# Attention into gated products: six token groups of 384 across batches instead of eight of 256 and 320

## The chip, the core and the metric

The kernel runs on one core of a Trainium2 chip. The metric is device time in microseconds (us). The engines are TensorE (PE; its weight loads are listed as PEld), VectorE (DVE), ScalarE (ACT), GpSimd (POOL) and SyncE (SP, which issues most DMAs).

## The reference

Three stages follow each other on 2304 tokens (4 batches of 576), in float32:

```python
scores = q @ k.T / 8                                  # 4 batches, 8 heads, 576 x 576, head dim 64
thresh = max(scores, -1) - tau
p = softmax(where(scores >= thresh, scores, -1e9))    # p / (sum + 1e-9)
x = (p @ v) as (2304, 512)
x = ((x @ w1) * (x @ w2) @ w3) @ w_out                # 512 -> 1024 -> 1024 -> 512
out = leaky(x @ w_in, 0.01) @ w_out2                  # 512 -> 2048 -> 512
```

## The kernel before

**Numbers.** Large products are made of float32r parts: a value is split into hi (a cast on ScalarE) and lo (value minus hi, on DVE or POOL), and each product takes three passes, hi hi, hi lo and lo hi (`PASSES`). Weights arrive as 64-bit words and are decoded in halves of 512 columns: ScalarE, DVE and POOL each have work in every half (L133 to L157).

**Attention.** Work goes by units: one batch, one pair of heads, one group of queries. A batch has two groups (`GROUPS`): queries 0 to 255 in two chunks of 128, and queries 256 to 575 as a tail of 64 (chunk `None`, both heads together) and two chunks of 128. A step is one chunk (`STEPS`, 80 in all, 64 chunks and 16 tails). In step n the kernel masks and normalises step n (`mask`), makes the scores of step n+1 (`scores`: matmuls, maximum on DVE, exponential on ScalarE), and transposes step n (`transposes`: four 128x128 transposes for each head into one PSUM tile `tp`, copied into `HH` by ScalarE for one head and by DVE for the other, and the ends of both heads through `tq` into `tl`). `mask` reads the scores in PSUM, and the score tiles are single, so the scores of the next step begin only when the mask of the one before has read them. The first 8 units (`PER`) use float32 scores, the later ones split q and k (`split_unit`). One step after a unit's last, `weighted` multiplies v^T by e (20 PE instructions, `av`) and splits the result out of PSUM into `x` (L349 on ScalarE, L350 on DVE).

**Filler.** The gated product of a group of tokens (`gated`) needs `x` of its four pairs of heads. It makes 16 sums of 12 matmuls (`psab`, L422), multiplies the two of each block (L430), splits the product into `gt` (L432, and L433 on POOL), and makes 4 sums of 24 matmuls (`psh`, L441), which go to DRAM as `h3d`. It is a generator that yields after each 12 matmuls (24 pieces a group). Two steps after the last step of a group it becomes the filler, and later steps draw pieces at 1.22 or 1.55 a unit of weight (a chunk weighs 2, a tail 1) at three places: behind `weighted`, between the two transposes, and behind them. Before the first group is ready, the places hold 16 pieces that fold w3 and w_out into `w34` (L388, 8 PE instructions each, two a step); a piece waits until the halves that it needs were decoded in earlier steps, and `load_halves` asks for 4 halves a step of the 40. Dummy matmuls (`keep_busy`, L496) run in the first three steps.

**Order.** The PE runs in the order in which the program is written. ACT, DVE and POOL are ordered by a planner in the attention part, and as written from the last gated group on. There, the last group's pieces (`last`) have no attention beside them; the work that prepares the second stage (`first_h3`, `prepare_up`, `prepare_down`) is drawn piece by piece beside them.

**Second stage.** 24 rounds of `products` (L861, 42 matmuls of 384 columns) and `down` (L896, 36 of 512 columns).

Of the kernel before, what the change touches and what calls it, by code (L numbers as in the profile page):

```python
# [44 lines left out]
def attention_gated_ffn(ctx: ExitStack, tc: tile.TileContext, qkv, tau, w3t, wout, w12, w2, out):  # L45
# [19 lines left out]
    xpool = s_ffn.enter_context(tc.tile_pool(name="xpool", bufs=6, reuse_waits="tile"))  # L65
# [95 lines left out]
    units = [(b * 4 + p, g) for b in range(B) for g in range(2) for p in range(4)]  # L161
    qk_t, vv_t = {}, {}

    def load_unit(u):

        if u >= len(units):
            return
        pair, g = units[u]
        gq, gw, _ = GROUPS[g]
        b, h = pair // 4, 2 * (pair % 4)  # L170
        qk = apool.tile([P, KS + 320], F32, tag="qk", name="qk", bufs=3)
        for a in range(2):
            o = a * D
            src = qkv[b, h + a][o:o + D]
            if g == 0:
                nc.sync.dma_start(out=qk[o:o + D, D:KS + gw], in_=src[:, :S + gw])
            else:
                nc.sync.dma_start(out=qk[o:o + D, D:KS], in_=src[:, :S])
                nc.sync.dma_start(out=qk[o:o + D, KS:], in_=src[:, S + gq:2 * S])
# [3 lines left out]
    def load_v(u):  # L183
        if u >= len(units):
            return
        pair = units[u][0]
        b, h = pair // 4, 2 * (pair % 4)
# [7 lines left out]
    def scale_unit(u):  # L195
# [3 lines left out]
        g = units[u][1]  # L199
        qk = qk_t[u]  # L200
        if g:
            for a in range(2):
                o = a * D
                tc.keep_in_program_order(nc.vector.tensor_scalar(
                    out=qz[u % 2][o:o + D, o:o + D], in0=qk[o:o + D, KS:KS + D], scalar1=scl[o:o + D],
                    scalar2=None, op0=ALU.mult))
        q = qk[:, KS + (D if g else 0):KS + GROUPS[g][1]]
# [5 lines left out]
    def split_unit(u):  # L213

        if not PER <= u < len(units):
            return
        g = units[u][1]
        n = KS + GROUPS[g][1]
# [9 lines left out]
        if g:  # L228
            for i, part in enumerate((hi, lo)):
                for a in range(2):  # L230
                    r = slice(a * D, a * D + D)
                    nc.vector.tensor_copy(qzs[u % 2][r, i, r], part[r, KS:KS + D])
# [4 lines left out]
    def scores(n):  # L237

        pair, g, c = STEPS[n]
        u = units.index((pair, g))  # L240
# [3 lines left out]
        if u < PER:  # L244
            parts, qzu = (qk,), qz[u % 2].unsqueeze(1)
        else:
            parts, qzu = qks_t[u], qzs[u % 2]
        passes = PASSES[:1] if u < PER else PASSES
        for half in range(2):
            for i, (x, y) in enumerate(passes):  # L250
                for a in heads:
                    if c is None:
                        lhs, rhs = qzu[:, x], parts[y][:, D + half * HS:D + half * HS + HS]
                    else:
                        r = slice(a * D, a * D + D)
                        o = KS + Q0[c] - GROUPS[g][0]
# [5 lines left out]
        nms = apool.tile([P, 2], F32, tag="nm", name="nm", bufs=4)  # L262
        th = apool.tile([P, 2], F32, tag="th", name="th", bufs=4)
# [8 lines left out]
        sc_t[n], e_t[n] = (sc, [th[:, a:a + 1] for a in heads]), e  # L272

    def mask(n):
        pair, g, c = STEPS[n]
        sc, ths = sc_t.pop(n)
        st = apool.tile([P, 2], F32, tag="stat", name="stat", bufs=4)
# [19 lines left out]
    def transposes(n):  # L297
# [3 lines left out]

        pair, g, c = STEPS[n]
        if (pair, g) not in he_t:
            he_t[pair, g] = apool.tile([P, 4, 2, 320], F32, tag="HH", name="HH")
        HH, tail = he_t[pair, g], tl[pair % 2]
# [14 lines left out]
        o = Q0[c] - GROUPS[g][0]  # L320
# [15 lines left out]
    def weighted(pair, g):  # L336

        gw = GROUPS[g][1]
        vv = vv_t[units.index((pair, g))]
        HH, tail = he_t.pop((pair, g)), tl[pair % 2]  # L340
# [646 lines left out]
```

## Time and profile before

| | us |
|---|---|
| median of 3 runs (lowest, highest) | 1034.69 (1030.94, 1035.38) |
| the profiled execution | 1033.24 |
| its span, first to last instruction | 1031.5 |
| PE busy | 1006.1 (98%) |
| DVE busy | 638.6 (62%) |
| ACT busy | 565.4 (55%) |
| POOL busy | 239.2 (23%) |

The mean granted clock of TensorE is 0.997 of full speed. Durations of single matmuls overlap, since they are pipelined; the distance from one start to the next is what a matmul costs when the PE is never idle. The chain that ended last goes mostly through L896 and L861, the second stage.

### The profile page before, as it was taken

What the parts mean: (1) busy time and instruction counts of PE and PEld (TensorE: products, weight loads), DVE (VectorE), ACT (ScalarE), POOL (GpSimd) and SP (SyncE); (2) the same over time, 40 slices, a digit from 0 to 9 for tenths busy, and PEclk for the clock granted to TensorE, in tenths of its full rate; (3) what the DMA queues carried; (4) which work ended last, traced back from release to release, by engine and by line L of the source; (5) the groups of instructions that cost most, each with busy time, mean ns of one, the idle gap of its engine ahead of it and who ended that gap; (6) DMA issues with size and microseconds to landing.
All of it is one profiled execution on the core that took longest, in us unless ns stands there. A gap on an engine that the chain in (4) does not pass through costs nothing. (4 is left out here: it accounts for less than half of the span.)

```text
span 1031.5 us, 17439 instructions
## 1 busy us (share of the span) xinstructions
PE 1006.1 (98%) x6472; PEld 862.6 (84%) x6472; DVE 638.6 (62%) x1394; ACT 565.4 (55%) x1084; POOL 239.2 (23%) x235
## 2 busy tenths in 40 slices
PE   7999899999999999999999999999999999999998
PEld 5555588889888888888898899998988999999997
DVE  7888788776787667887767856476683111621111
ACT  5778755554565545565545646677874333543332
POOL 2556510010110110100101135344552111411110
PEclk9999999999999999999999999999999999999999
DMA  8666211312121212112110225678645952064401
GB/s 291 229 218 218 69 50 40 108 43 62 44 59 53 62 37 62 49 44 69 45 49 20 73 83 188 225 300 281 211 147 194 424 195 95 1 242 192 189 1 62
DMA packets 53284, 129.59 MB, mean 126 GB/s; under 512 B 15824, under 2 KB 31184, under 8 KB 49360
## 3 DMA queue, kind: packets, MB, share of 16 engines
q1 hardware_dynamic: 53056, 128.48, 36.2%
q8 instruction: 51, 0.84, 0.3%
q14 instruction: 33, 0.27, 0.1%
q10 hardware_dynamic: 144, 0.00, 0.0%
HBM read 95.95 MB, written 32.51 MB: 125 GB/s over the span
## 5 line engine op out<-in xcount | busy, mean ns | idle before, releaser
L422 PE MATMUL psab<-x,w 128*128 128x256 f32 (+1 forms) x1536 | 232.4, 302 | 2.0 <-DVE w L394 0.5
L422 PEld LDWEIGHTS psab<-x,w 128*128 128x128 f32 x1536 | 208.7, 189 | 18.4 <-issue 10.3
L896 PE MATMUL po<-dn,gg 128*128 128x512 f32 x864 | 222.9, 390 | 0.0
L896 PEld LDWEIGHTS po<-dn,gg 128*128 128x128 f32 x864 | 160.1, 188 | 22.0
L861 PE MATMUL ps<-h,uph 128*128 128x384 f32 x672 | 172.9, 339 | 1.4 <-DVE sum L843 0.6
L267 ACT ACTIVATE e<-sc,nm 128x576 f32<-128x576 f32 x144 | 100.9, 738 | 82.8 <-DVE nm L266 81.9
L266 DVE TENSOR_REDUCE nm<-sc 128x1 f32<-128x576 f32 x144 | 103.2, 752 | 65.5 <-PE sc L259 65.4
L843 DVE TENSOR_TENSOR sum<-snap,ps 128x384 f32<-128x384 f32 x72 | 39.8, 552 | 167.1 <-PE ps L861 157.0
L861 PEld LDWEIGHTS ps<-h,uph 128*128 128x128 f32 x672 | 123.4, 188 | 15.7 <-DVE sum L843 1.4
L433 POOL TENSOR_TENSOR gt<-at,gt 128x256 fp32r<-128x256 f32 (+1 forms) x64 | 52.5, 820 | 340.2 <-ACT gt L432 340.0
L280 DVE SCALAR_TENSOR_TENSOR e<-sc,th,e 128x576 f32<-128x576 f32 x144 | 113.2, 814 | 12.5 <-ACT e L267 8.9
L441 PE MATMUL psh<-gt,w 128*128 128x256 f32 (+1 forms) x768 | 114.9, 301 | 1.3 <-POOL gt L433 1.3
L861 PE MATMUL ps<-h,upl 128*128 128x384 f32 x336 | 113.2, 337 | 0.0
L441 PEld LDWEIGHTS psh<-gt,w 128*128 128x128 f32 x768 | 103.9, 189 | 6.5 <-issue 3.5
L851 POOL TENSOR_TENSOR gg<-sum,gg 128x384 fp32r<-128x384 f32 x48 | 50.5, 1052 | 248.1 <-ACT gg L850 230.3
L325 PE MATMUL tp<-ident,e 128*128 128x128 f32 x512 | 78.5, 276 | 10.9 <-ACT HH L331 10.0
L838 ACT COPY snap<-ps 128x384 f32<-128x384 f32 x72 | 34.3, 476 | 86.8 <-PE ps L861 86.6
L325 PEld LDWEIGHTS tp<-ident,e 128*128 128x128 f32 x512 | 61.2, 142 | 21.5 <-ACT HH L331 14.0
L346 PE MATMUL av<-HH,vv 128*64 128x256 f32 (+1 forms) x512 | 67.6, 406 | 0.0
L848 ACT ACTIVATE sum<-sum 128x384 f32<-128x384 f32 x72 | 37.8, 525 | 48.1 <-DVE sum L843 48.1
L861 PEld LDWEIGHTS ps<-h,upl 128*128 128x128 f32 x336 | 63.1, 188 | 0.0
L291 ACT ACTIVATE e<-e,stat 128x576 f32<-128x576 f32 x64 | 49.7, 777 | 23.8 <-DVE stat L285 23.5
(116 smaller groups left out, 1399.2 us busy)
## 6 DMA issues: line engine op xcount, KB each, us to landing
st<-in_w SPq DMA_DIRECT2D x48, 512.0 KB, 5.9
dn<-dn_d SPq DMA_DIRECT2D x10, 1024.0 KB, 7.2
uph<-up_d SPq DMA_DIRECT2D x10, 896.0 KB, 9.2
upl<-up_d SPq DMA_DIRECT2D x10, 896.0 KB, 4.6
vv<-in_qkv SPq DMA_DIRECT2D x64, 128.0 KB, 2.1
raw<-in_w3t SPq DMA_DIRECT2D x8, 1024.0 KB, 7.6
dn_d<-dn SPq DMA_DIRECT2D x8, 1024.0 KB, 6.9
up_d<-uph SPq DMA_DIRECT2D x8, 896.0 KB, 4.6
```

Of the source, the lines that this page charges most:

```text
L266: nc.vector.tensor_reduce(out=nm, in_=sc[a][:, :, :HS], op=ALU.max, axis=AX.XY, negate=True)
L267: nc.scalar.activation(e[:, a * S:a * S + S].rearrange("p (a b) -> p a b", a=2), sc[a][:, :, :HS], AF.Exp, bias=nm)
L280: nc.vector.scalar_tensor_tensor(out=ev, in0=sc[a][:, :, :HS], scalar=th, in1=ev, op0=ALU.is_ge, op1=ALU.mult, accum_out=st[:, a:a + 1])
L291: nc.scalar.activation(ev, ev, AF.Copy, scale=st[:, a:a + 1])
L325: nc.tensor.transpose(tp[:, kc], e[:, k0:k0 + P], ident)
L346: nc.tensor.matmul(av[a * D:a * D + D, :gw], vv[:, a, kc], rhs, start=(i == 0), stop=(i == NK - 1))
L422: nc.tensor.matmul(ps[:, :gw], w12_t[i][:, a, mat * 512 + kk * P:mat * 512 + kk * P + P], xt[kk][:, c, :gw], start=(m == 0), stop=(m == 11))
L433: nc.gpsimd.tensor_tensor(out=gt[i][:, 1, :gw], in0=at[:, :gw], in1=f(gt[i][:, 0, :gw]), op=ALU.subtract)
L441: nc.tensor.matmul(ps[:, :gw], w34_t[i // 2][:, a, i % 2, o * P:o * P + P], gt[i][:, c, :gw], start=(m == 0), stop=(m == 23))
L851: eng.tensor_tensor(out=gg[:, 1], in0=gf, in1=f(gg[:, 0]), op=ALU.subtract)
L861: nc.tensor.matmul(ps, (uph, upl)[a][:, wi, i * P:i * P + P], hs[k][:, c, i], start=(opens[k] and m == 0), stop=(m == 5), skip_group_check ...
L896: nc.tensor.matmul(po_t[o], gg[:, c, t * P:t * P + P], dn[:, i, a], start=(q == 0 and seen[o] == 1 and m == 0), stop=(q == NQ - 1 and seen ...
```

## The change

The queries of two batches that follow each other (1152 tokens) are cut into three groups of 384. The first is queries 0 to 383 of the even batch in three chunks; the second joins its last 192 (a tail of 64 and one chunk) to the first 192 of the odd batch (likewise); the third is the last 384 of the odd batch. There are 32 units and 80 steps as before, with 384 or 192 queries to a unit. The gated product runs for 6 groups of 384 tokens, each matmul 384 columns wide. `weighted` only copies `av` into a float32 tile `xr` of the group (on ScalarE); `split_x` makes hi and lo of all four tiles in front of `gated`. A gated generator yields after 6 matmuls (48 pieces a group), and says whether a sum is open; open sums are finished ahead of `weighted`. The rate is 2.04, `load_halves` asks for 3 halves a step, `qz`, `tl` and `qzs` are single, intermediate tiles of the last group come from `fpool` too, the first two rings of the second stage trade places, and preparation for it is drawn at every second piece. The rest of the diff (not shown) puts the new names and widths in place of the old ones.

```diff
-Q0 = (0, 128, 320, 448)
-GROUPS = ((0, 256, (0, 1)), (HF, 320, (2, 3)))
 NK = 5
-CHUNKS = ((0, 1), (None, 2, 3))
-STEPS = tuple(
-    (b * 4 + p, g, c) for b in range(B) for g in range(2) for p in range(4) for c in CHUNKS[g])
+GW = 384
+NG = NT // GW
+PARTS = (
+    ((0, 384, (0, 128, 256)), (384, 192, (None, 64))),
+    ((0, 192, (None, 64)), (192, 384, (0, 128, 256))))
+UNITS = tuple(
+    (b + i, p, g) for b in range(0, B, 2)
+    for several in (((0, 0),), ((0, 1), (1, 0)), ((1, 1),)) for p in range(4) for i, g in several)
+STEPS = tuple((u, c) for u, (b, p, g) in enumerate(UNITS) for c in PARTS[b % 2][g][2])
...
-    xpool = s_ffn.enter_context(tc.tile_pool(name="xpool", bufs=6, reuse_waits="tile"))
+    xpool = s_ffn.enter_context(tc.tile_pool(name="xpool", bufs=4, reuse_waits="tile"))
...
-    qz = [apool.tile([P, P], F32, name=f"qz{i}") for i in range(2)]
-    tl = [apool.tile([P, 320], F32, name=f"tl{i}") for i in range(2)]
+    qz = apool.tile([P, P], F32, name="qz")
+    tl = apool.tile([P, GW], F32, name="tl")
     vvs = [apool.tile([P, 2, NK, D], F32, name=f"vv{i}") for i in range(2)]
-    for t in (*qz, *tl, *(vv[:, :, NK - 1] for vv in vvs)):
+    for t in (qz, tl, *(vv[:, :, NK - 1] for vv in vvs)):
         nc.vector.memset(t, 0.0)
-    qzs = [apool.tile([P, 2, P], F32R, name=f"qzs{i}") for i in range(2)]
-    for t in qzs:
-        nc.vector.tensor_copy(t, tl[0][:, :2 * P].rearrange("p (a w) -> p a w", a=2))
+    qzs = apool.tile([P, 2, P], F32R, name="qzs")
+    nc.vector.tensor_copy(qzs, tl[:, :2 * P].rearrange("p (a w) -> p a w", a=2))
...
+    def piece_of(u):
+
+        b, p, g = UNITS[u]
+        gq, gw, blocks = PARTS[b % 2][g]
+        at = b * S + gq
+        return gq, gw, blocks[0] is None, at // GW, at % GW
...
+        few = apool.tile([P, 6], F32, tag="nm", name="nm", bufs=4)
+        nms, th = few[:, :2], few[:, 2:4]
...
-        x = x_t[pair, g] = xpool.tile([P, 2, 320], F32R, tag="x", name="x")
-        nc.scalar.copy(x[:, 0, :gw], av[:, :gw])
-        nc.vector.tensor_tensor(
-            out=x[:, 1, :gw], in0=av[:, :gw], in1=f(x[:, 0, :gw]), op=ALU.subtract)
-
+        if (gid, p) not in x_t:
+            x_t[gid, p] = xpool.tile([P, GW], F32, tag="xr", name="xr")
+        nc.scalar.copy(x_t[gid, p][:, at:at + gw], av[:, :gw])
+
+    def split_x(gid):
+
+        xt = []
+        for p in range(KD):
+            raw = x_t.pop((gid, p))
+            x = xpool.tile([P, 2, GW], F32R, tag="x", name="x")
+            nc.scalar.copy(x[:, 0], raw)
+            nc.vector.tensor_tensor(out=x[:, 1], in0=raw, in1=f(x[:, 0]), op=ALU.subtract)
+            xt.append(x)
+        return xt
...
-        if tail:
-            return p2.tile([P, 320], F32, tag="os", name=name, bufs=3)
-        return fpool.tile([P, 320], F32, tag="at", name=name)
-
-    def gated(b, g):
-
-        gq, gw, _ = GROUPS[g]
-        xt = [x_t.pop((b * 4 + p, g)) for p in range(KD)]
+        return fpool.tile([P, GW], F32, tag="at", name=name)
...
+    def gated(gid, xt):
+
         gt = {}
         for i in range(KF):
             while halves_of(both[i]) + 2 > halves_in[0]:
                 load_halves(1)
             for mat in range(2):
-                ps = bank("psab")
+                ps = bank("psab")[:, :GW]
                 m = 0
                 for kk in range(KD):
                     for a, c in PASSES:
                         nc.tensor.matmul(
-                            ps[:, :gw], w12_t[i][:, a, mat * 512 + kk * P:mat * 512 + kk * P + P], xt[kk][:, c, :gw],
+                            ps, w12_t[i][:, a, mat * 512 + kk * P:mat * 512 + kk * P + P], xt[kk][:, c],
                             start=(m == 0), stop=(m == 11))
                         m += 1
+                    if kk == 1:
+                        yield True
                 if mat == 0:
                     at = spare("at")
-                    nc.scalar.copy(at[:, :gw], ps[:, :gw])
-                    yield
-            nc.vector.tensor_tensor(out=at[:, :gw], in0=ps[:, :gw], in1=at[:, :gw], op=ALU.mult)
-            gt[i] = gpool.tile([P, 2, 320], F32R, tag="g", name="gt")
-            nc.scalar.copy(gt[i][:, 0, :gw], at[:, :gw])
-            nc.gpsimd.tensor_tensor(
-                out=gt[i][:, 1, :gw], in0=at[:, :gw], in1=f(gt[i][:, 0, :gw]), op=ALU.subtract)
-            yield
+                    nc.scalar.copy(at, ps)
+                    yield False
+            nc.vector.tensor_tensor(out=at, in0=ps, in1=at, op=ALU.mult)
+            gt[i] = gpool.tile([P, 2, GW], F32R, tag="g", name="gt")
+            nc.scalar.copy(gt[i][:, 0], at)
+            nc.gpsimd.tensor_tensor(out=gt[i][:, 1], in0=at, in1=f(gt[i][:, 0]), op=ALU.subtract)
+            yield False
...
+                if i % 2 and i < KF - 1:
+                    yield True
             ht = spare("ht")
-            nc.scalar.copy(ht[:, :gw], ps[:, :gw])
-            nc.sync.dma_start(out=h3d[o, :, b * S + gq:b * S + gq + gw], in_=ht[:, :gw])
-            yield
+            nc.scalar.copy(ht, ps)
+            nc.sync.dma_start(out=h3d[o, :, gid * GW:gid * GW + GW], in_=ht)
+            yield False
...
+    open_ = [False]
+
+    def more(k):
+
+        for _ in range(k):
+            open_[0] = next(filler, False)
...
-        kh = 2 if n == 0 else 4
+        kh = 2 if n == 0 else 3
...
+        if weigh:
+            while open_[0]:
+                more(1)
+                due -= 1
+            weighted(weigh.pop())
+        k = max(0, int(due))
         due -= k
         parts = [(k + 2) // 3, (k + 1) // 3, k // 3]
...
-        if last_of_unit and pair % 4 == 3:
-            queue.append((n + 2, pair // 4, g))
+        if last_of_unit and (n == NS - 1 or piece_of(u + 1)[3] != gid):
+            queue.append((n + 2, gid))
...
-            filler = gated(b, gg)
-            rate, due = (1.22, 1.55)[gg], 0.0
-    weighted(*weigh.pop())
+            filler = gated(gid, split_x(gid))
+            rate, due, open_[0] = 2.04, 0.0, False
+    while open_[0]:
+        more(1)
+    weighted(weigh.pop())
+    xt = split_x(NG - 1)
     s_att.close()
...
-            ring[n] = ring[n - 3] if n >= 3 else ("wB", "wA", "w34")[n]
+            ring[n] = ring[n - 3] if n >= 3 else ("wA", "wB", "w34")[n]
...
-    early = [(start, 1, 9), (prepare_up(0), 10, 17), (prepare_up(1), 16, 23), (prepare_down(0), 20, 24)]
+    early = [(start, 1), (prepare_up(0), 18), (prepare_up(1), 28), (prepare_down(0), 40)]
     for i, _ in enumerate(last):
-        for gen, a, z in early:
-            if a <= i + 1 <= z:
+        for gen, a in early:
+            if a <= i + 1 and (i + 1 - a) % 2 == 0:
                 run(gen, 1)
-    for gen, _, _ in early:
+    for gen, _ in early:
```

## Rows read from the trace of the kernel before

**Rows 1.** Stretches: us, then busy us (instructions) by engine, PEclk, DMA share, GB/s.
```profile
0.00:114.76 114.76, 105.51 (x462) 61.47 (x463) 93.06 (x195) 85.97 (x153) 58.08 (x51) 0.97 0.68 228
114.76:602.17 487.41, 477.63 (x3805) 415.21 (x3803) 370.18 (x920) 260.10 (x498) 53.72 (x76) 1.00 0.19 54
652.00:1031.50 379.50, 374.38 (x1872) 337.66 (x1870) 145.24 (x235) 193.06 (x380) 102.26 (x88) 1.00 0.48 181
```

**Rows 2.** PE in order of time, end of attention: start, us, line, operation, count.
```profile
602.17 6.01 PE L441 MATMUL psh<-gt,w 128*128 128x256 f32 x48
608.02 28.32 PE L422 MATMUL psab<-x,w 128*128 128x320 f32 x192
636.18 3.39 PE L441 MATMUL psh<-gt,w 128*128 128x320 f32 x22
...
652.32 0.51 PE L861 MATMUL ps<-h,uph 128*128 128x384 f32 x2
...
655.80 0.34 PE L861 MATMUL ps<-h,upl 128*128 128x384 f32 x1
```

**Rows 3.** PE in order of time, attention of the second batch.
```profile
244.88 0.65 PE L346 MATMUL av<-tl,vv 128*64 128x256 f32 x4
...
247.19 2.02 PE L441 MATMUL psh<-gt,w 128*128 128x320 f32 x12
...
283.75 0.76 PE L346 MATMUL av<-tl,vv 128*64 128x320 f32 x4
...
286.59 1.70 PE L422 MATMUL psab<-x,w 128*128 128x256 f32 x12
288.13 0.60 PE L312 MATMUL tp<-ident,e 128*128 128x128 f32 x4
```

**Rows 4.** Groups by line, whole span: busy us, mean ns | idle before.
```profile
L851 DVE TENSOR_TENSOR gg<-sum,gg 128x384 fp32r<-128x384 f32 x24 | 13.3, 553 | 2.4 <-ACT gg L850 2.3
...
L350 DVE TENSOR_TENSOR x<-av,x 128x256 fp32r<-128x256 f32 (+1 forms) x32 | 14.4, 450 | 3.2 <-ACT x L349 3.2
```

**Rows 5.** PE in order of time, the front.
```profile
12.69 0.66 PE L325 MATMUL tp<-ident,e 128*128 128x128 f32 x4
...
21.00 1.12 PE L325 MATMUL tp<-ident,e 128*128 128x128 f32 x4
...
34.57 0.60 PE L325 MATMUL tp<-ident,e 128*128 128x128 f32 x4
...
38.11 1.24 PE L259 MATMUL sc<-qk 64*128 64x288 f32 x8
...
44.84 1.30 PE L259 MATMUL sc<-qk 64*128 64x288 f32 x8
...
52.84 0.60 PE L325 MATMUL tp<-ident,e 128*128 128x128 f32 x4
53.27 3.60 PE L388 MATMUL ps<-wo,w 128*128 128x512 f32 x8
56.71 0.60 PE L325 MATMUL tp<-ident,e 128*128 128x128 f32 x4
...
58.52 3.70 PE L388 MATMUL ps<-wo,w 128*128 128x512 f32 x8
62.06 0.60 PE L325 MATMUL tp<-ident,e 128*128 128x128 f32 x4
...
114.76 0.50 PE L422 MATMUL psab<-x,w 128*128 128x256 f32 x1
```

**Rows 6.** All engines in order of time, one row of DVE.
```profile
44.02 0.81 DVE L280 SCALAR_TENSOR_TENSOR e<-sc,th,e 128x576 f32<-128x576 f32 x1
```

**Rows 7.** Stretches of PE: us, busy us (instructions), PEclk, DMA share, GB/s.
```profile
18.00:20.00 2.00, 0.24 (x2) 1.00 0.99 386
22.00:24.00 2.00, 1.02 (x5) 0.50 0.86 281
```

**Rows 8.** PE's longest wait from 114.76 to 130 us: total, times, longest.
```profile
PE tp L325 <- ACT HH L331: 2.1, 1, 2.1
```

More of the change, by code (lines that the diff above doesn't have):

```diff
@@ L159, in stream @@
         return decode(), issue
-    units = [(b * 4 + p, g) for b in range(B) for g in range(2) for p in range(4)]
     qk_t, vv_t = {}, {}
+    def piece_of(u):
[3 more added lines that the diff above has]
+        return gq, gw, blocks[0] is None, at // GW, at % GW
     def load_unit(u):
-        if u >= len(units):
+        if u >= len(UNITS):
             return
-        pair, g = units[u]
-        gq, gw, _ = GROUPS[g]
-        b, h = pair // 4, 2 * (pair % 4)
-        qk = apool.tile([P, KS + 320], F32, tag="qk", name="qk", bufs=3)
+        b, p, _ = UNITS[u]
+        gq, gw, _, _, _ = piece_of(u)
+        h = 2 * p
+        qk = apool.tile([P, KS + GW], F32, tag="qk", name="qk", bufs=3)
         for a in range(2):
@@ L183, in load_v @@
     def load_v(u):
-        if u >= len(units):
+        if u >= len(UNITS):
             return
-        pair = units[u][0]
-        b, h = pair // 4, 2 * (pair % 4)
+        b, p, _ = UNITS[u]
+        h = 2 * p
         vv = vv_t[u] = vvs[u % 2]
@@ L198, in scale_unit @@
             return
-        g = units[u][1]
+        _, gw, tailed, _, _ = piece_of(u)
         qk = qk_t[u]
-        if g:
+        if tailed:
             for a in range(2):
@@ L213, in split_unit @@
     def split_unit(u):
-        if not PER <= u < len(units):
+        if not PER <= u < len(UNITS):
             return
-        g = units[u][1]
-        n = KS + GROUPS[g][1]
+        _, gw, tailed, _, _ = piece_of(u)
+        n = KS + gw
         qk = qk_t[u]
@@ L231, in split_unit @@
                     r = slice(a * D, a * D + D)
-                    nc.vector.tensor_copy(qzs[u % 2][r, i, r], part[r, KS:KS + D])
+                    nc.vector.tensor_copy(qzs[r, i, r], part[r, KS:KS + D])
     sc_t, e_t = {}, {}
     def scores(n):
-        pair, g, c = STEPS[n]
-        u = units.index((pair, g))
+        u, c = STEPS[n]
         qk = qk_t[u]
@@ L244, in scores @@
         if u < PER:
-            parts, qzu = (qk,), qz[u % 2].unsqueeze(1)
+            parts, qzu = (qk,), qz.unsqueeze(1)
         else:
-            parts, qzu = qks_t[u], qzs[u % 2]
+            parts, qzu = qks_t[u], qzs
         passes = PASSES[:1] if u < PER else PASSES
@@ L297, in transposes @@
     def transposes(n):
[L302 to L305, printed above, removed]
+        u, c = STEPS[n]
+        if u not in he_t:
+            he_t[u] = apool.tile([P, 4, 2, GW], F32, tag="HH", name="HH")
+        HH, tail = he_t[u], tl
         e = e_t.pop(n)
@@ L334, in attention_gated_ffn, with weighted @@
     x_t = {}
[L336 to L340, printed above, removed]
+    def weighted(u):
+        _, gw, _, gid, at = piece_of(u)
+        p = UNITS[u][1]
+        vv = vv_t[u]
+        HH, tail = he_t.pop(u), tl
         av = ps_w.tile([P, 512], F32, tag="w", name="av")
@@ L518, in attention_gated_ffn @@
             scores(n + 1)
-        if n and STEPS[n - 1][:2] != (pair, g):
+        if n and first_of_unit:
             split_unit(u + 1)
         due += rate * weight
-        k = int(due)
+        if weigh:
[4 more added lines that the diff above has]
+        k = max(0, int(due))
         due -= k
@@ L526, in fill @@
         def fill(i):
-            run(filler, parts[i])
+            more(parts[i])
             if i < 2:
                 fold_some(1, decoded)
-        if weigh:
-            weighted(*weigh.pop())
         fill(0)
@@ L809, in attention_gated_ffn @@
         mybir.EngineType.Activation, mybir.EngineType.DVE, mybir.EngineType.Pool, mybir.EngineType.SP}))
-    last = chain(filler, gated(B - 1, 1))
+    last = chain(filler, gated(NG - 1, xt))
     issue()
```

50 lines of the change are left out of this document (22 added, 28 removed).

## The prediction

> **What bounds the kernel now.** I read the table of stretches first [rows 1]. From 114.76 us to the end TensorE (PE) is busy for 98 to 99% of the time (477.63 of 487.41 us, 374.38 of 379.50 us), so there a microsecond of PE work is a microsecond of kernel. Before 114.76 us it is busy for 105.51 us, and part of that is dummy work (L496). VectorE (DVE) is busy for 370.18 of 487.41 us in the middle (76%) and 93.06 of 114.76 us (81%) in front. Then the PE's order in time [rows 2, 3]: the reader is to see that one run of matmuls begins where the one before it ends, so the distance between starts is the price of a matmul, whose own duration overlaps its neighbours. Last the front of the timeline [rows 5 to 7], where there is no gated product yet to fill the PE.
>
> So the change has to be costed as PE starts, and as PE idle in the front.
>
> **Fewer, wider gated matmuls.** A group has 8 x 24 matmuls on L422 and 4 x 24 on L441: 288. Before: 4 groups of 256 and 4 of 320 columns, 1152 matmuls of each; after: 6 x 288 = 1728 of 384. Spacings [rows 2]: 256 columns, (608.02 - 602.17)/48 = 121.9 ns; 320 columns, (636.18 - 608.02)/192 = 146.7 ns. The second stage already has 384 columns: 20 matmuls lie between 652.32 and 655.80 us, 174.0 ns each. Before: 1152 x (121.9 + 146.7) ns = 309.4 us; after: 1728 x 174.0 ns = 300.7 us; **-8.7 us**. If the slope from 256 to 320 held on, 384 columns would take 171.5 ns and the saving be 13.1 us: the far bound. The near bound is nothing saved, which is a rival below.
>
> A page weighs against this saving. The Trainium skill ("TensorE: Matmul & The Clock Gate", section "Back-to-back issue gap") gives the isolated gap at full clock as N/2.4 ns plus about 2.5 ns, whatever the width. By it 576 matmuls fewer save an estimated 1.4 us instead of 8.7. The spacings here are 10.9 to 12.7 ns longer than that formula at all three widths, so the trace does not agree, and the measured spacings decide.
>
> **Attention work.** It stays at 32 units, 64 chunks of 128 queries and 16 tails. The weighted product takes 247.19 - 244.88 = 2.31 us at 256 columns and 286.59 - 283.75 = 2.84 us at 320 [rows 3]; 0.53 us per 64 columns makes 3.37 at 384 and 1.78 at 192, and 16 of each cost as before: 0. Bound: if an instruction could not follow the last in less than the 0.11 us of a transpose (four from 52.84 to 53.27) [rows 5], the narrow ones would cost 16 x 20 x 0.02 = 6 us more; I take 0, because that 0.43 us holds a change of kind of work, and the two measured widths lie on the line. Units of 384 and 192 queries load and split 1024 and 832 columns instead of 896 and 960, the same sum; K and V go through SP's queue 32 times as before, at a DMA share of 0.19 in the middle [rows 1], hidden.
>
> **More changes between gated work and attention.** A run of 12 matmuls of 256 columns takes 288.13 - 286.59 = 1.54 us [rows 3], where 12 x 121.9 ns is 1.46: about 0.08 us for each change. Before, some 170 runs lie inside attention (2.4 to 3.1 pieces a chunk step); after, 4.08 half-size pieces a chunk step fall into three runs each, and a tail step has two: some 184. 14 x 0.08 = **+1.1 us** (0 to +2). The run between the two transposes of a step shrinks from 12 matmuls (1.5 to 1.8 us) to 6 (1.05 us). ScalarE's copy must fit in it. It does while ScalarE (260.10 of 487.41 us busy) is not inside the exponentials, and the run ahead of the first transpose grows to 12 x 0.174 us, which gives those more time: 0, with the bound in the range.
>
> **The front.** This is the term that decides. The first group's attention now has 12 steps, not 8; the filler starts two steps after its last, so with step 14 instead of step 10. Until then only 16 folding pieces fill the PE, about 3.5 us each (53.27 to 56.71) [rows 5], and with three half-weights decoded a step instead of four they come later: none in step 3, one in 9, two in the others from 4 to 11, none in 12 and 13.
>
> A step with two pieces takes 62.06 - 52.84 = 9.2 us [rows 5] and is full. A chunk step without pieces has 0.43 + (58.52 - 56.71) = 2.24 us of PE work [rows 5], but its length is set by scores, maximum, exponential, mask, next scores: scores start at 38.11 and 44.84 us, the second right as DVE's mask ends at 44.02 + 0.81 [rows 5, 6], so 6.7 us. Step by step, as times of the first transpose: step 1 at 21.0 as now; step 2 at 34.57 - 2.3 (no weighted product yet) = 32.3; step 3 (weighted product for a piece) +8.2 = 40.5; step 4 +6.7 = 47.2; step 5 +9.2 = 56.4; step 6 +9.2 + 3.4 = 69.0; 7 and 8 to 87.4; 9 to 100.0; 10, short, 106.7; 11 115.9; 12 (pieces only at its start, then the weighted product) 125.0; 13 +3.7 behind a tail, 128.7. Scores of step 15 wait for the mask of 14 (about 131), then 1.2 us, then 1.8 us of weighted product: the filler starts near **134** instead of 114.76, 19.3 us later. By then more PE work is done: four chunks 4 x 2.24 = 9.0, and 4 x 3.37 + 1.78 - 4 x 2.31 = 6.0 of weighted products, 15.0 in all. The rest is new idle: **+4.3 us**, taken as +5 for copies that come late between the two transposes. Bounds: at 8.3 us (12.69 to 21.00) [rows 5] for the four short steps it is +11; if DVE alone paced it (93.06 us and four chunk steps of some 5 us, 113 us in a front of 130, 87% busy), 0.
>
> PE is then about half busy from 125 to 131 us. After such a stretch (0.24 us busy of 2 at 18 us) the granted clock stood at 0.50, the 1.2 GHz level, at 22 us [rows 7]; in the middle it is 1.00, in front 0.97, which is (1 - 0.97) x 114.76 / 0.5 = 6.9 us at half [rows 1]. A second such spell would cost half of it: 0 to +3.4, taken as **+1.5**.
>
> In the other direction, the wait of 2.1 us for one of ScalarE's copies just behind 114.76 us [rows 8] falls where ScalarE is still decoding; decoding is over at step 14: **-2** (-2.1 to 0).
>
> **v^T e in float32, split later.** Removed: 32 subtractions on DVE out of PSUM (450 ns) [rows 4]. Added: 24 casts and 24 subtractions of 384 columns; the same form takes 553 ns on DVE [rows 4]. They stand together in front of a group: 4 x 0.55 = 2.2 us of DVE in one step. Queued behind them on DVE are that step's masks, and behind those the next scores. DVE has 370.18 us for 70 steps in the middle [rows 1], 5.3 us a step, and a chunk step without weighted product will last about 6.3 us, so some 1.2 us would show if all four stood there; three of the four inputs are ready a unit or more earlier and DVE has 24% free. Four switches in attention x 0.5 = **+2** (0 to +6). At the last one some 7 pieces of the group before (7 x 1.05 us) cover it: 0. If they were gone, PE would wait some 3 us.
>
> **The end and the second stage.** Shared tail buffers (qz, qzs, tl) are each read by the PE ahead of the next write: 0. The last gated group stays PE-bound, its POOL subtraction a little longer: +0.2. In the second stage PE is idle for 5.1 of 379.5 us [rows 1] and its work is unchanged; other ring tags and earlier preparation move at most 2 us: 0.
>
> **Sum:** -8.7 + 1.1 + 5 + 1.5 - 2 + 2 + 0.2 = **-0.9 us**. It stands against the profiled execution, 1033.24 us (span 1031.5), so 1032.3. The median of the runs is 1.45 us higher than that execution: **1034**.
>
> **Rivals.** A difference of 0.5% (5.2 us) is about what a measurement of this kernel can tell from no change.
> - A, the forecast: the front gives back what the wider matmuls save. 1034, within 1030 to 1039. Chance 0.47.
> - B, the front hides: three decodes a step instead of four shorten its chain, the idle and the clock spell stay away, the splits go into DVE's free time. The sum becomes -8.7 + 1.1 - 2 + 0.2 = -9.4, or 1025; with one of these terms left, 1028. For it: DVE and ScalarE have a fifth of the front free. Against: PE already stalled there with fewer attention steps. Chance 0.30.
> - C, slower: the short steps take 8.3 us and the clock falls: -0.9 + 6 + 2 = +7.1, or 1042. It decides as soon as idle and clock together exceed 12.6 us instead of 6.5. For it: early steps did take 8.3 us. Against: fewer decodes per step. Chance 0.18.
> - D, wider saves nothing: at 309.4/1728 = 179 ns for 384 columns the saving is gone, and the time 1034 + 8.7 = 1042.7; growing in proportion from 121.9 ns, they would take 183. Against: 174.0 ns measured, in a stage without fp32 transposes between. The page named above would put it near there, at 1041. Chance 0.05.
>
> Faster by over 0.5%: B, 0.30. Same: A, 0.47. Slower: C and D, 0.23. The range takes A, most of B down to 1024, and C up to 1044, which leaves out the corners in which all bounds fall together.
>
> **What would show it.** Gated matmuls at 174 ns or less and 1728 of them; first gated matmul near 134 us (before 130: B; after 139: C); granted clock below 1 between 125 and 140 us; no PE wait on casts of x at group switches of more than 1 us; last gated matmul to end of kernel unchanged near 380 us. The prediction fails if the middle turns DVE-bound (busy over 90% there), or if copies between transposes stall the PE each step: 52 chunk steps at 0.2 us would add 10 us.

## The result, and the profile after

The changed kernel takes 1048.19 us (median of 6 runs, 1044.59 to 1049.30), the kernel before, beside it, 1032.85 us (6 runs, 1030.81 to 1036.32): ratio 1.0141, 95% interval 1.0113 to 1.0168. It is slower, by 4 us more than the range allowed. The profiled execution took 1044.59 us (span 1042.8).

Stretches of the changed kernel, with the columns of [rows 1]: the front up to the first gated matmul, from there to the end of the last weighted product, and the second stage.

```profile
0.00:146.22 146.22, 125.27 (x550) 70.79 (x550) 118.69 (x239) 102.68 (x182) 62.02 (x55) 0.94 0.55 179
146.22:605.34 459.12, 448.24 (x3141) 384.45 (x3139) 348.80 (x850) 251.06 (x452) 45.76 (x56) 1.00 0.19 55
663.74:1042.80 379.06, 374.34 (x1873) 337.92 (x1872) 145.11 (x235) 193.09 (x380) 102.13 (x88) 1.00 0.47 178
```

The gated work begins at 146.22 us, 31.5 us later than before and 12.2 us later than forecast. PE's order in time where attention ends, as in [rows 2]:

```profile
611.69 2.24 PE L455 MATMUL psh<-gt,w 128*128 128x384 f32 x12
613.77 33.44 PE L435 MATMUL psab<-x,w 128*128 128x384 f32 x192
647.05 16.85 PE L455 MATMUL psh<-gt,w 128*128 128x384 f32 x96
663.74 0.51 PE L890 MATMUL ps<-h,uph 128*128 128x384 f32 x2
```

192 matmuls in 33.28 us are 173.3 ns each: the price of a wide matmul is as forecast. Held against the sum, for the profiled executions:

| stretch | before, us | after, us | forecast of the difference | measured |
|---|---|---|---|---|
| start to first gated matmul | 114.76 | 146.22 | +21.5 (15.0 of moved work, 6.5 lost) | +31.5 (16.5 lost) |
| from there to the first product of the second stage | 537.04 | 517.52 | -22.4 | -19.5 |
| second stage to the end of the span | 379.70 | 379.06 | 0 | -0.6 |
| span | 1031.5 | 1042.8 | -0.9 | +11.3 |

Ten of the 12.2 us between forecast and span are lost in front. The median lies 3.6 us above the profiled execution, where the forecast added 1.45 (mean granted clock 0.988 to 0.989 in the other executions, 0.992 in this one). PE in the front, at some of its steps and where the gated work was due:

```profile
40.33 0.66 PE L332 MATMUL tp<-ident,e 128*128 128x128 f32 x4
43.93 0.66 PE L332 MATMUL tp<-ident,e 128*128 128x128 f32 x4 [2.94 <-ACT HH L338]
...
49.33 0.60 PE L332 MATMUL tp<-ident,e 128*128 128x128 f32 x4
...
102.36 0.60 PE L332 MATMUL tp<-ident,e 128*128 128x128 f32 x4
...
109.09 0.60 PE L332 MATMUL tp<-ident,e 128*128 128x128 f32 x4
...
112.96 0.60 PE L332 MATMUL tp<-ident,e 128*128 128x128 f32 x4
113.40 0.27 PE L335 MATMUL tq<-ident,e 128*128 128x128 f32 x1
113.77 1.24 PE L267 MATMUL sc<-qk,qz 128*128 128x288 f32 x4
117.05 5.40 PE L405 MATMUL ps<-wo,w 128*128 128x512 f32 x8 [2.04 <-POOL w L152]
122.29 0.60 PE L332 MATMUL tp<-ident,e 128*128 128x128 f32 x4
...
126.60 0.27 PE L335 MATMUL tq<-ident,e 128*128 128x128 f32 x1
126.80 1.24 PE L267 MATMUL sc<-qk 64*128 64x288 f32 x8
...
131.35 0.66 PE L319 MATMUL tp<-ident,e 128*128 128x128 f32 x4
131.84 0.27 PE L320 MATMUL tq<-ident,e 128*128 128x128 f32 x1
136.18 2.26 PE L267 MATMUL sc<-qk,qz 128*128 128x288 f32 x4 [4.07 <-issue]
138.23 1.06 PE L332 MATMUL tp<-ident,e 128*128 128x128 f32 x4
...
146.22 0.98 PE L435 MATMUL psab<-x,w 128*128 128x384 f32 x4
```

Folding at 117 us waits for a weight that GpSimd has not finished, and a run of 8 then takes 5.40 us where it took 3.60 before [rows 5]: half clock for part of it (PEclk is 0.79 from 114 to 122 us, and 0.57 from 138 to 146). Then PE stands still for 4.07 us before the scores at 136.18. PE's largest waits up to 147 us (us in total, times, longest):

```profile
PE tp L332 <- ACT HH L338: 9.4, 6, 2.9
PE sc L267 <- issue: 4.1, 1, 4.1
```

The first is for ScalarE's copy between the two transposes of a step; it was 4.3 us in the front of the kernel before. The stretch before the late scores on the other engines:

```profile
129.69 0.44 DVE L149 TENSOR_SCALAR t<-t 128x512 int32<-128x512 int32 x1
130.05 0.68 DVE L157 TENSOR_TENSOR w<-lw,w 128x512 fp32r<-128x512 f32 x1
130.31 1.55 POOL L155 TENSOR_TENSOR lw<-t,lw 128x512 int32<-128x512 int32 x1 [0.47 <-ACT lw L148]
130.65 1.24 DVE L278 TENSOR_SCALAR nm<-nm,cb 128x2 f32<-128x2 f32 x1
...
134.05 1.27 POOL L155 TENSOR_TENSOR lw<-t,lw 128x512 int32<-128x512 int32 x1 [0.64 <-DVE nm L291]
...
134.57 1.06 DVE L296 TENSOR_SCALAR e<-e,nm 128x576 f32<-128x576 f32 x1
...
135.55 0.53 DVE L213 TENSOR_SCALAR qz<-qk,scl 64x64 f32<-64x64 f32 x2
```

The scores at 136.18 need `qz`, which DVE makes at 135.55 behind the masks of step 13. DVE is late for two reasons: weights are still being decoded here (L149, L157), and two of its instructions end just behind an instruction of POOL (130.65 + 1.24 = 131.89, POOL at 131.86; 134.57 + 1.06 = 135.63, POOL at 135.32). The first of them has two elements.

In the middle PE has one new wait (us in total, times, longest), which stands for 10 starts of a two-step unit with a tail, on `qzs`, the split q that is made last on DVE:

```profile
PE sc L267 <- DVE qzs L241: 7.2, 20, 1.3
```

### The profile page after: what moved, and what is told of

The parts are those of the page before. It is cut to its first block, busy times and chain, and to the rows that moved or that the text cites. A ratio compares the mean times of both kernels' runs of the same rounds, so it can differ in the third digit from the quotient of the medians.

```text
span 1042.8 us, 16142 instructions
## 1 busy us (share of the span) xinstructions
PE 1006.2 (96%) x5896; PEld 851.5 (82%) x5896; DVE 644.2 (62%) x1367; ACT 574.5 (55%) x1068; POOL 235.3 (23%) x219
## 5 line engine op out<-in xcount | busy, mean ns | idle before, releaser
L435 PE MATMUL psab<-x,w 128*128 128x384 f32 x1152 | 233.6, 346 | 0.0
L435 PEld LDWEIGHTS psab<-x,w 128*128 128x128 f32 x1152 | 195.7, 188 | 11.4 <-DVE e L287 5.4
L448 POOL TENSOR_TENSOR gt<-at,gt 128x384 fp32r<-128x384 f32 x48 | 50.2, 1045 | 376.3 <-ACT gt L447 376.3
L287 DVE SCALAR_TENSOR_TENSOR e<-sc,nm,e 128x576 f32<-128x576 f32 x144 | 113.1, 815 | 13.5 <-ACT e L275 8.7
L455 PE MATMUL psh<-gt,w 128*128 128x384 f32 x576 | 114.1, 344 | 0.0
L455 PEld LDWEIGHTS psh<-gt,w 128*128 128x128 f32 x576 | 98.1, 188 | 4.8 <-issue 2.4
L332 PEld LDWEIGHTS tp<-ident,e 128*128 128x128 f32 x512 | 63.5, 141 | 26.9 <-ACT HH L338 13.0
L298 ACT ACTIVATE e<-e,nm 128x576 f32<-128x576 f32 x64 | 49.7, 777 | 40.8 <-DVE nm L292 40.3
L334 DVE COPY HH<-tp 128x512 f32<-128x512 f32 x64 | 44.2, 690 | 39.5 <-PE tp L332 39.4
L354 PE MATMUL av<-HH,vv 128*64 128x384 f32 (+1 forms) x512 | 67.6, 406 | 0.0
```

The source lines that it names most:

```text
L287: nc.vector.scalar_tensor_tensor(out=ev, in0=sc[a][:, :, :HS], scalar=th, in1=ev, op0=ALU.is_ge, op1=ALU.mult, accum_out=st[:, a:a + 1])
L298: nc.scalar.activation(ev, ev, AF.Copy, scale=st[:, a:a + 1])
L332: nc.tensor.transpose(tp[:, kc], e[:, k0:k0 + P], ident)
L354: nc.tensor.matmul(av[a * D:a * D + D, :gw], vv[:, a, kc], rhs, start=(i == 0), stop=(i == NK - 1))
L435: nc.tensor.matmul(ps, w12_t[i][:, a, mat * 512 + kk * P:mat * 512 + kk * P + P], xt[kk][:, c], start=(m == 0), stop=(m == 11))
L448: nc.gpsimd.tensor_tensor(out=gt[i][:, 1], in0=at, in1=f(gt[i][:, 0]), op=ALU.subtract)
```

## The experiments

Each ratio is to the kernel before on the same chip; 0.001 of it is 1.03 us, and differences between experiments are taken from the ratios.

**The front by itself.** Theory F: the front loses because its folding is spread badly and the gated work starts late. Paced folding:

```diff
-            if i < 2:
+            if i < 2 and folded[0] < (n - 1) * 4 / 3:
                 fold_some(1, decoded)
```

> Kernel after, with the 16 folding pieces of the front held back to about 1.33 a step, so that steps 9 to 13 have one too; nothing else is changed. Theory F (the loss is PE idle in the front, steps 11 to 14, and the half clock that follows from it): the idle and the half-clock stretch between 114 and 146 us go, the first gated matmul starts at 132 to 137 us instead of 146, and the time falls by 9 to 15 us, to about that of the kernel before or a little under. Theory T (the loss is in the middle, in the waits for the single tail tiles qzs): the first gated matmul may come earlier, but the time stays within 3 us of the changed kernel, 1.2% over the kernel before.

1052.20 us, 1.0174 (1.0142 to 1.0207). The first gated matmul came at 158.09 us; the waits for ScalarE's copy between the two transposes of a step grew to 16.4 us, from 9.4. F fell in this form. Dummy matmuls in steps 11 to 13 (`keep_busy`; 8, 14 and 8 of them):

> Kernel after, with dummy 128x128 matmuls into a spare bank in the idle places of steps 11, 12 and 13 (8, 14 and 8 of them); the kernel's own work is unchanged. If the half clock is the larger part of what the front lost (theory F, clock): granted clock at least 0.995, time down by 5 to 8 us. If idle alone is the price (theory F, idle): clock up, time down by at most 2 us. Theory T: no more than 2 us either way.

1048.83 us, 1.0147 (1.0121 to 1.0173). PEclk was 1.00 from 110 to 150 us, the first gated matmul came at 145.61 us, and the time was the same: ending the half clock in this way gains nothing. What it costs by itself is not shown, since the dummies take PE time too.

**Single tiles.** Theory T: sharing them costs the time. The kernel before, with one `qz`, `tl` and `qzs` instead of two of each:

> Kernel before, with one tile each for qz, qzs and tl instead of two; nothing else is changed. Theory T in the form that single tiles cause the waits: PE waits for qzs of 5 to 10 us appear and the time rises by as much, 0.5 to 1%. Theory F: no change beyond 2 us, since each tile is read before the next write comes up.

1033.95 us, 1.0012 (0.9998 to 1.0026). They cost nothing; T fell.

**Half-weights decoded in a step.** One line of the change undone:

```diff
-        kh = 2 if n == 0 else 3
+        kh = 2 if n == 0 else 4
```

> Kernel after, with four half-weights decoded a step as before instead of three. If decoding that comes too late is what starves the front: no wait for a decoded half at 117 us, shorter steps 12 and 13, time down by 4 to 8 us. If the front lacks PE work for its steps (theory F, idle): the folding is used up two steps earlier, idle only moves forward, time within 3 us of the changed kernel or above it.

1041.43 us, 1.0079 (1.0052 to 1.0105): 6.4 us less, with the first gated matmul at 144.48 us. The profiled executions differ by only 2.4 us (spans 1040.4 and 1042.8), 1.7 of them in front; where the rest of the 6.4 lies is not shown. And three instead of four in the kernel before (with its v^T e split as in f3, below):

> The kernel before with v^T e in float32 and split in front of its group, and three half-weights decoded a step instead of four. Theory K (three halves cost their 7 us only because the front of the changed kernel has 12 steps of attention and too little folding to fill them): 8 steps of 3 leave the folding short by a few pieces, which the gated work then waits for: 1029 to 1033. Rival (three a step cost the same wherever they stand): 1034 to 1037.

1039.70 us, 1.0059 (1.0038 to 1.0080), against 0.9956 with four: 10.6 us. The first gated matmul moved from 113.64 to 125.13 us. Theory K, which held that only the long front pays, fell: both fronts pay, and the time lies above the rival's range too.

**The front as before, wide groups behind it.**

```diff
-NG = NT // GW
...
+WIDTHS = (256, 320, 384, 384, 384, 256, 320)
...
+RATES = (2.45, 2.04, 2.04, 2.04, 3.06, 2.45)
+NG = 7
```

> Everything of the changed kernel but the cut into groups at both ends: batch 0 and batch 3 keep groups of 256 and 320 tokens, batches 1 and 2 share three of 384; four halves decoded a step. So the front has 8 steps as in the kernel before, and half of the gated matmuls are 384 wide. Gated matmuls: 576 x (121.9 + 146.7) + 864 x 174.0 ns = 305.0 us, 4.4 less than before. Theory F (the front's four added steps are the price): first gated matmul back near 115 us, time 1028 to 1033, no slower than before. Theory M (the middle of the changed kernel, with wide pieces, two-step units and splits in front of a group, is the price): still 4 us or more above the kernel before.

1041.63 us, 1.0081 (1.0063 to 1.0098), with the first gated matmul at 112.72 us. The expected 1028 to 1033 failed: what the front no longer lost, the rest did (PE waits 4.0 us for `qzs` and 4.3 for `gt` behind the attention, PEclk is 0.87 from 625 to 650 us, and 190 runs of gated work lie inside attention, where there were 160). Theory M's range, 4 us or more above the kernel before, came true. First gated work one step earlier (and its rate 1.9, not 2.04), on the six groups with four halves:

```diff
-            queue.append((n + 2, gid))
+            queue.append((n + (2 if gid else 1), gid))
```

> Kernel after with four halves decoded a step, and the first group's gated product handed to the filler one step sooner (behind step 12, not 13). Beside the run with four halves alone (1041.4 us): theory F: first gated matmul 5 to 8 us earlier, time down by 4 to 7 us, to 1034 to 1037. Theory M: within 2 us of 1041.

1041.94 us, 1.0084 (1.0068 to 1.0100). It began at 139.38 instead of 144.48 us and all of it was given back: from there to the second stage took 5.0 us longer.

**v^T e in float32, by itself** (of the change, this part alone, in the kernel before):

```diff
-        nc.scalar.copy(x[:, 0, :gw], av[:, :gw])
-        nc.vector.tensor_tensor(
-            out=x[:, 1, :gw], in0=av[:, :gw], in1=f(x[:, 0, :gw]), op=ALU.subtract)
+        x_t[pair, g] = xpool.tile([P, 320], F32, tag="xr", name="xr")
+        nc.scalar.copy(x_t[pair, g][:, :gw], av[:, :gw])
...
```

> Kernel before with one part of the change alone: v^T e kept in float32 and split in front of its group (32 casts and 32 subtractions of 256 or 320 columns, four at a time). Theory F: 0 to +2 us. Theory M, in the form that the splits hold DVE up at each group: +5 us or more, with PE waits on x or on scores just behind each of the seven switches.

1028.81 us, 0.9956 (0.9940 to 0.9971): 4.5 us faster than before, outside both expectations. In the kernel before, all engines in order of time:

```profile
194.35 2.02 PE L422 MATMUL psab<-x,w 128*128 128x320 f32 x12
195.22 0.38 ACT L349 CAST x<-av 128x256 fp32r<-128x256 f32 x1
196.47 0.42 ACT L428 COPY at<-psab 128x320 f32<-128x320 f32 x1 [0.86 <-PE psab L422]
196.61 0.41 DVE L350 TENSOR_TENSOR x<-av,x 128x256 fp32r<-128x256 f32 x1
196.94 0.74 PEld L422 LDWEIGHTS psab<-x,w 128*128 128x128 f32 x5 [0.37 <-ACT at L428]
```

There are two PSUM tiles for `psab` and `av`. ScalarE has read `av` by 195.60, but DVE's subtraction holds the tile until 197.02; the next `psab` starts at 196.94, right behind the copy of the `psab` before it (196.47 + 0.42 = 196.89), so it took the other tile and waited for that copy. Nine such waits of the weight loads, 3.3 us in all, are gone with the subtraction. Of the 4.6 us between the profiled spans, 2.8 lie between the first gated matmul and the second stage and 1.1 before that; that the tile accounts for all of it is not shown.

**The split q and k of the two-step units**, made in another order (`qzs` from the scaled q, ahead of the wide split; four halves):

> Kernel after with four halves decoded a step, and the tail tile qzs made from the scaled q itself, ahead of the wide split, so that its four DVE instructions wait for nothing late. Beside the run with four halves alone (1041.4 us): if the 7.2 us of PE waits for qzs are time lost, they go and the time falls by 5 to 7 us; if the PE would have waited for something else there, waits move and the time changes by less than 2 us.

1041.84 us, 1.0089 (1.0063 to 1.0115), like e4. The wait moved to the next thing that DVE makes:

```profile
PE sc L268 <- DVE qkl L241: 5.8, 10, 0.6
```

**The finer pieces.** The cut that the change makes, alone in the kernel of f3; and undone, in e4 and in f1:

```diff
+                    if kk == 1:
+                        yield True
...
-                if i == 3:
-                    yield
+                if i % 2 and i < KF - 1:
+                    yield True
```

> The kernel before with v^T e in float32 and split in front of its group (1028.8 us when run alone), and on top of it only the finer cut of the gated work: pieces of 6 matmuls instead of 12, twice the rate. Theory P (what the middle lost is the cutting: each change from a gated run into scores cost about 0.2 us and into transposes 0.1 us, and there are some 30 more runs): 1033 to 1037. Rival S (the middle lost only what the two-step units wait for their own split q and k): no two-step units here, so 1028 to 1031.

> The changed kernel with four half-weights a step (1041.4 us) and pieces of 12 matmuls instead of 6, half the rate: two pieces of about 2.2 us in a chunk step, behind scores and between the two transposes, none in front of the next scores. Theory P: fewer changes, 1035 to 1039. Rival S: 1040 to 1043. If the step without a third piece exposes the masks, it is over 1043.

> The kernel with groups of 256, 320, 384, 384, 384, 256 and 320 columns (its front as before, 1041.6 us), with pieces of 12 matmuls instead of 6. Theory P: the 30 more runs go away, 1033 to 1037. Rival S: the two-step units are still there, 1040 to 1043.

1034.19 us, 0.9998 (0.9984 to 1.0012): 4.3 us over f3, with 185 runs inside attention instead of 160. 1039.93 us, 1.0066 (1.0040 to 1.0092): 1.3 us under e4, inside the noise, with 117 runs instead of 179. 1038.81 us, 1.0047 (1.0032 to 1.0063): 3.5 us under f1, short of the forecast. P holds on the old groups; on six equal groups it can't be told from S. What a change looks like, in PE's order in time of the changed kernel:

```profile
154.20 1.30 PE L435 MATMUL psab<-x,w 128*128 128x384 f32 x6
155.34 0.60 PE L332 MATMUL tp<-ident,e 128*128 128x128 f32 x4
155.78 0.27 PE L335 MATMUL tq<-ident,e 128*128 128x128 f32 x1
155.81 1.30 PE L435 MATMUL psab<-x,w 128*128 128x384 f32 x6
157.03 1.24 PE L267 MATMUL sc<-qk 64*128 64x288 f32 x8
```

Six matmuls at 174.0 ns are 1.04 us: into transposes a run takes 0.10 us on top, into scores 0.18. But the run in front of scores starts 0.03 us behind the single transpose before it (155.78, 155.81), where scores in its place start 0.20 us behind it (126.60, 126.80, above): 0.17 of its 0.18 us is given back at its start. That fits g3, which drops this run of each chunk step and gains so little. With 25 more runs in g1, 0.10 us each would be 2.5 of the 4.3 us; the rest is open.

**Folding in half-size pieces, one in each place of a step; dummies behind f2; both together.** All with four halves:

```diff
-                if j == 3:
+                if j % 2 and j < KF - 1:
                     yield
...
-            if i < 2:
-                fold_some(1, decoded)
+            fold_some(1, decoded)
```

> The changed kernel with four half-weights a step (1041.4 us, first gated matmul at 144.5 us), and the folding cut into 32 pieces of half the size, one in each of a step's three places, so that it lasts until step 12. Theory E (bare steps behind a folding that is used up too early hold the front): first gated matmul at 133 to 138 us, 1031 to 1036. Rival V (VectorE's chain paces the twelve steps): 141 us or later, 1039 to 1043.

> The kernel whose first gated work starts one step earlier (1041.9 us, first gated matmul at 139.4 us, the granted clock 0.79 between 130 and 146 us), with 22 dummy matmuls in each of steps 11 and 12. If the half clock behind the bare steps took what the earlier start gave: clock 1.00 there and 1037 to 1040. If not: 1041 to 1043.

> The finer, even folding together with the start of the gated work one step earlier. Theory E: first gated matmul at 129 to 134 us and 1029 to 1035, as the first of these runs or somewhat faster. Rival V: first gated matmul at 137 us or later, 1039 to 1043.

1048.73 us, 1.0150 (1.0133 to 1.0168), first gated matmul at 149.16; 1045.62 us, 1.0119 (1.0103 to 1.0134), at 143.36; 1048.36 us, 1.0141 (1.0120 to 1.0161), at 146.32. Theory E failed in both its runs, and all three times lie above the rival's range as well. In the first, PE's waits before 150 us are longer than with whole folding pieces (e4: 6.3 us for the copy):

```profile
PE tp L332 <- ACT HH L338: 12.2, 9, 2.6
PE sc L267 <- DVE qk L218: 8.8, 4, 3.1
```

The dummies held PEclk at 1.00 from 130 to 146 us (0.79 without) and cost more than they gave. The waits that grew are for ScalarE and DVE, so the last experiments look there.

**VectorE and GpSimd in the front.** DVE in the changed kernel, by form, in front (first three rows) and from 146.22 to 605.34 us (last three): busy us, mean ns, idle before.

```profile
L287 DVE SCALAR_TENSOR_TENSOR e<-sc,nm,e 128x576 f32<-128x576 f32 x28 | 22.4, 814 | 1.7
L296 DVE TENSOR_SCALAR e<-e,nm 128x576 f32<-128x576 f32 x15 | 11.6, 776 | 0.3
L278 DVE TENSOR_SCALAR nm<-nm,cb 128x2 f32<-128x2 f32 x13 | 9.1, 700 | 0.4
...
L287 DVE SCALAR_TENSOR_TENSOR e<-sc,nm,e 128x576 f32<-128x576 f32 x116 | 90.7, 815 | 11.9 <-ACT e L275 8.7 <-DVE nm L278 0.5
L296 DVE TENSOR_SCALAR e<-e,nm 128x576 f32<-128x576 f32 x65 | 33.8, 519 | 2.0
L278 DVE TENSOR_SCALAR nm<-nm,cb 128x2 f32<-128x2 f32 x51 | 12.1, 237 | 1.8
```

Two of these forms are slow where POOL is busy, and the mask (L287) is not. The Trainium skill ("SBUF — State Buffer", section "Who interferes with whom") says that copies, casts and tensor-scalar instructions can take a pair of ports shared with GpSimd, and that whoever comes second waits for the other's whole instruction. The trace agrees: the two tensor-scalar forms take 700 and 776 ns in front, 237 and 519 ns behind it, and L287, which is of another kind, keeps its 815 ns.

Three runs. In two of them, on e4 and on f3, two elements are given as one and one and the second head's scaling is moved to ScalarE, in the first eight units. In the third, on e4 alone, seven eighths of POOL's additions of the low words are left out (its output is not the reference's):

```diff
-        nc.vector.tensor_scalar(
-            out=th[:, :m], in0=nms[:, :m], scalar1=-1.0, scalar2=cb, op0=ALU.mult, op1=ALU.add)
+        for x in [slice(a, a + 1) for a in heads] if u < PER else [slice(0, m)]:
+            nc.vector.tensor_scalar(
+                out=th[:, x], in0=nms[:, x], scalar1=-1.0, scalar2=cb, op0=ALU.mult, op1=ALU.add)
...
-            if a == m - 1:
+            if a == m - 1 and not few_dve(n):
...
-                    nc.gpsimd.tensor_tensor(out=lw, in0=t, in1=lw, op=ALU.add)
+                    nc.gpsimd.tensor_tensor(out=lw[:, :64], in0=t[:, :64], in1=lw[:, :64], op=ALU.add)
```

> The changed kernel with four half-weights a step (1041.4 us, first gated matmul at 144.5 us), whose two-element instructions of VectorE are given as single elements and whose scaling of the second head's exponentials moves from VectorE to ScalarE, in the first eight units. Theory L (VectorE's instructions wait for GpSimd's to end, and that stretches the chain of each step in the front): first gated matmul at 137 to 141 us, 1034 to 1039. Rival A (ScalarE's copies between the transposes pace the front, and get another 12 us of work in front of them): 144 us or later, 1041 to 1046.

> The kernel before with v^T e in float32 and split in front of its group (1028.8 us, first gated matmul at 113.6 us), with the same edit. Theory L: the front has a step less to lose, 1025 to 1028. Rival A: 1029 to 1033.

> The changed kernel with four half-weights a step, in which GpSimd adds the low words of only 64 of each 512 columns of the weights decoded in the front (7 in 8 are left out, so that the output is not the reference's): 40 instructions of 1.3 us become short. Theory L: VectorE's two-element instructions return to about 240 ns and its scaling to about 520 ns, the first gated matmul comes at 132 to 139 us, 1029 to 1036. Rival A: the first gated matmul at 142 us or later, 1039 to 1042.

1033.41 us, 0.9995 (0.9986 to 1.0004), first gated matmul at 138.00; **1022.12 us, 0.9890 (0.9875 to 0.9904)**, at 110.86, the fastest version, 1.1% under the kernel before; 1037.05 us, 1.0031 (1.0019 to 1.0044), at 141.66. In the third run (first row) two elements, which took 813 ns in e4, are back at 223 ns, in the first (second row) single ones take 206:

```profile
L281 DVE TENSOR_SCALAR nm<-nm,cb 128x2 f32<-128x2 f32 x14 | 3.1, 223 | 0.2
...
L279 DVE TENSOR_SCALAR nm<-nm,cb 128x1 f32<-128x1 f32 x30 | 5.7, 206 | 0.1
```

The edit is worth 8.7 us in the changed kernel with four halves and 6.8 us on the old groups, both beyond L's range; 6.5 and 2.8 us of these appear before the first gated matmul. The third run gained 5.0 us and misses L's range on the other side: its collisions on these two forms are all but gone (223 ns, and 567 for the scaling, which took 1140 in e4), and its front is only 2.8 us shorter. So L holds in part. That the first run does more suggests that the scaling moved off DVE counts beside the collision; the two were not taken apart.

## Why the prediction was wrong

**Failed: the front.** The step "That is +4.3 us of new idle, taken as +5", with its +1.5 for the clock, measured 16.5 us. By [rows 1] and the first stretch above, PE stands still for 20.95 us in front where it did for 9.25, 11.7 us more; and it is busy 19.8 us longer for 15.0 us of moved work, 4.8 us more, at a granted clock of 0.94 instead of 0.97. The step allowed 0.7 us for copies late between transposes; they grew by 5.1 us (4.3 to 9.4). The late scores cost 4.1 us and the late weight 2.0. Its times for the first transposes hold to 2.4 us up to step 10 (109.09 us, forecast 106.7); then step 11 comes at 122.29 (115.9; 13.2 us behind step 10 where 9.2 were due), 12 at 131.35 (125.0), 13 at 138.23 (128.7). Two things were left out of these last steps, as the runs show:
- Three half-weights a step. The forecast let them delay the folding pieces and counted them as a relief for the chain (rival B). Early on they are one: step 3 begins at 40.33 us, with four halves (e4) at 47.82. But decoding then still occupied ScalarE, DVE and POOL when the gated work was due. In all it cost 6.4 us here (e4) and 10.6 us on the old groups (g2).
- The chain of the last steps. Of the short steps, costed at 6.7 us, one took 6.7 (102.36 to 109.09) and one 9.0 (40.33 to 49.33, behind the wait of 2.94 us for a copy). Behind the tail the steps were costed at 3.7 and 5.3 us, little more than PE's work; they took 6.9 and 8.0 us (131.35, 138.23, 146.22): in the first PE stood 4.07 us behind DVE, whose instructions wait for POOL's, and in the second 1.25 us behind ScalarE's copy, at a granted clock of 0.57. The collision of DVE and POOL is in both kernels, so it is no cost of the change by itself: with the edit in both, 10.8 us remain between them (0.9995 against 0.9890).

With four halves and the collision out of the way, the gated work starts at 138.00 us, 4 us after the forecast, 8.2 us are lost in front where 6.5 were forecast, and the kernel takes 1033.4 us where 1034 was forecast. That agreement is luck in part: the edit is worth 6.8 us on the old groups too, and the forecast did not have it.

**Rival C** had the right sign, and its condition came true: idle and clock passed 12.6 us, with the first gated matmul after 139. Its four short steps of 8.3 us took 9.0, 6.7, 6.9 and 8.0. Its price, 1042, was too low by 6 us; it had nothing for the 4.0 us more between steps 10 and 11.

**Right: the wide matmuls.** 173.3 ns measured for 174.0. Rival D is refuted by the same rows. So is the saving of 1.4 us by the Trainium skill ("TensorE: Matmul & The Clock Gate", section "Back-to-back issue gap"), whose formula for the isolated gap gives an estimated 162.5 ns at 384 columns.

**Wrong in sign: the split.** +2 us was taken for bursts of splits at group switches. Alone, the part gains 4.5 us: what the trace shows gone is not DVE time but the hold on a PSUM tile, 1.4 us in the row shown. No row of the forecast looked at who holds a tile that PE wants next. If the gain holds on the new groups, which no run tests, most of it lies inside the changed kernel's way from 537.04 to 517.52 us.

**Undersized: changes, and DVE's order.** 179 runs lie inside attention instead of 160 (forecast: 14 more); a run's end takes 0.10 or 0.18 us instead of 0.08, most of the 0.18 given back, and the finer cut cost 4.3 us on the old groups, where the forecast had +1.1 for its own. "Shared tail buffers: 0" was right (e3), but the units of two steps start 7.2 us late on their split q and k, which no step of the sum had. The whole middle came out 2.9 us above the forecast.

**Right: attention work** (a weighted product of 384 columns takes 3.38 us and one of 192 takes 1.78; forecast 3.37 and 1.78), **the end and the second stage** (-0.6 us).

**Open.** Between e4 and f3, equal but for grouping, pieces and tiles, the new front still loses 15.8 us beyond its extra work (12.1 between j1 and j2). So this loss of the change itself is not explained. That the last steps run bare when folding is used up is seen; that this is the cause was not shown, since spreading the folding, dummies and an earlier start each failed to bring it back. Making the split of q and k a unit earlier was not tried.

## What to carry to other kernels

A stage that fills an engine from other work has a second resource, the chain of small instructions that releases each step; before giving such a stage more steps, read what each small instruction costs there and where the chip is quiet, form by form. An operation that reads PSUM a second time is to be priced by how long the tile stays taken and who wants it next, not by its own duration. And a saving per instruction, however well measured, is only the first line of the sum: here it came out to within 1 ns, and the time went the other way.

## What the runs showed of the hardware

- A two-element tensor-scalar instruction on DVE took 700 ns on average in the front, where POOL was decoding (813 ns in e4; the one shown took 1.24 us), 237 ns behind it, and 223 ns in front once most of POOL's additions were cut short (j3); single elements took 206 ns in the same front (j1). The mask, of another kind, kept 815 ns.
- A run of 6 gated matmuls takes 0.10 us more in front of transposes and 0.18 us more in front of scores, but the run in front of scores starts 0.17 us sooner than the scores would have.
- Filling PE's idle time with dummies brought the granted clock from 0.79 to 1.00 in a stretch of 16 us, and the kernel still became 3.6 us slower.
